# Attention in front of two expert layers on one core: array shapes of the attention matmuls

## The chip, the cores and the metric

One core of a Trainium2 chip runs the whole program. The metric is the device time of one execution in microseconds. Before the change three runs took 944.69, 947.47 and 947.21 us; their median is 947.21.

## The reference

Causal attention over 4 batches, 8 heads, 576 positions and head size 64, with a decay bias, then two feed-forward layers on the 2304 tokens:

```python
scores = scale * np.matmul(q, k.transpose(0, 1, 3, 2))
bias = -(cum[:, :, :, None] - cum[:, :, None, :])          # cum: running sum of max(s, 0)
scores = np.where(causal, -1000000000.0, scores + np.minimum(bias, 0.0))
attn = np.exp(scores - np.max(scores, axis=-1, keepdims=True))
attn = attn / (np.sum(attn, axis=-1, keepdims=True) + 1e-09)
x = np.matmul(attn, v)                                     # heads side by side: 2304 x 512
h = x @ w_in                                               # 512 -> 2048
x = (h * np.clip(h + 3.0, 0.0, 6.0) / 6.0) @ w_out         # 2048 -> 512
h = np.maximum(np.maximum(x @ w1, x @ w2), x @ w3)         # 512 -> 768
out = h @ w_out2                                           # 768 -> 512
```

All inputs are float32. The weights are decoded on the chip from 64-bit words.

## The kernel before, in words

The 576 queries of a head are cut into five chunks of up to 128; the last one, chunk 4, has 64 (n in the code). A "slot" (lines 839 to 927) handles one chunk of one head: TensorE (PE) makes its scores in PSUM (ps_s, line 865), the queries being the stationary operand and the keys the moving one; VectorE adds the causal mask and finds the row's extreme (line 886); ScalarE takes the exponential and sums the row (line 894); PE transposes the result in pieces of 128 keys (pt, line 916); ScalarE copies it to the tile e1p or e2p (batch 0) or e1, e2 (later batches). "average" (lines 929 to 976) multiplies it with the values (px, lines 948 and 955) for the first two chunks (group 0, 256 queries) or the last three (group 1, 320 queries). "reciprocals" turns the row sums into 1/sum and spreads each over 64 columns (ex); "finish" transposes that (pt_r, line 1014), multiplies the averages by it and stores the result (x_d). Two heads that lie side by side are a pair, and their averages are the two halves of 128 rows.

Batch 0 differs from the later ones. Its scores and averages are plain float32 matmuls, of which each shows as two records of PE in the trace. The later batches split every operand into a rounded float32 and its rest; a score there is two matmuls with one record each (128 and 66 rows), and an average has the rounded value and its rest side by side as 128 stationary columns. In batch 0 an average has the 64 values of one head as stationary columns. The scores of chunk 4 have 64 stationary columns in every batch, its transposes and the transposes of its reciprocals have 64 rows. All other matmuls use 128*128 or 66*128 (rows*columns of the stationary operand).

Between the attention's instructions PE does the first expert layer for tokens that are ready ("three", lines 484 to 488; ps_h and ps_x), and in the first 60 us some idle matmuls (line 574). The order of all instructions on every engine is fixed when the program is built: a planner (class Flow) runs the threads against costs that are written in the code (each `yield` with an engine and a cost) and emits an instruction when its engine comes free in the plan. On the chip each engine works through its list in order and waits on semaphores.

Rows of the sums that chunk 4 does not fill were set to 1 at the start (line 594), and the columns behind the 576 keys in chunk 4's tile e4 were set to 0 (line 596), on its 64 rows.

Of the kernel before, what the change touches and what calls it, by code (L numbers as in the profile page):

```python
# [15 lines left out]
AF = mybir.ActivationFunctionType  # L16
# [4 lines left out]
B, H, S, D = 4, 8, 576, 64  # L21
NT, DM, DFF, DF2 = B * S, 512, 2048, 768
P = 128
# [4 lines left out]
NCH = 5  # L28
U1 = S // 2
UCUT = ((0, 2 * P), (2 * P, S))  # L30
# [271 lines left out]
def attn_moe_moe2(ctx, tc, q, k, v, s, w_in, w_out, w1, w2, w3, w_out2, out):  # L302
# [187 lines left out]
    CHUNKED = ((0, 1), (2, 3, 4))  # L490
# [63 lines left out]
    def part_of(b, c):  # L554
        return min(1, c // 2) if b == 0 else 0
# [28 lines left out]
    def setup():  # L584
        make_identity(nc, ident)
        pool.memset(above, 0.0)
        pool.affine_select(
            out=above[:, 4 * P:], in_=above[:, 4 * P:], pattern=[[-1, P]],
            compare_op=ALU.is_ge, fill=MASK, base=0, channel_multiplier=1,
        )  # L590
        vec.memset(half, 0.5)
        for z in range(3):
            sums_of[z] = ap.tile([P, 2 * NCH], F32, tag=f"sums{z}", name="sums", bufs=1)
            vec.memset(sums_of[z], 1.0)
        e4 = ap.tile([P, NCH * P], F32, name="e4", bufs=1)
        pool.memset(e4[:S - 4 * P, S:], 0.0)
        et[0, "e4"] = e4
        et[0, 0] = ap.tile([P, 2, 2, 256], F32, tag="e1", name="e1p", bufs=1)
        et[0, 1] = ap.tile([P, 2, NCH, 320], F32, tag="e2", name="e2p", bufs=1)
        warm = psa.tile([P, P], F32, tag="t0", name="warm", bufs=1)  # L600
        for n in range(WARM):
            pe.matmul(warm, lhsT=ident, rhs=ident, start=(n == 0), stop=(n == WARM - 1))
# [236 lines left out]
    def slot(i, item, tiny):  # L839
        b, p, j, c = seq[i]  # L840
        h, pr = heads[b, p, j], pair[b, p, part_of(b, c)]
        n = min(P, S - c * P)
        qs = slice(c * P, c * P + n)
        soon = b == 0
        if soon:
            z, *tiles = yield early[part_of(b, c), p]
            o = c * P - UCUT[part_of(b, c)][0]
            passes = [(tiles[0][:, j, o:o + n], tiles[1][:, j])]
        else:
            passes = [(lhs[:, qs], rhs) for lhs, rhs in (yield h.ready)]  # L850
        w = min(S, (c + 1) * P)
        wp = (w + P - 1) // P * P
        e = et[0, "e4"] if c == NCH - 1 else make(item, [P, 512], F32, "e")
        cuts = [(0, 288), (288, 576)] if w > 512 else [(0, w)]
        parts = []
        for lo, hi in cuts:
            bank = yield S_.get()
            ps = make(bank, [P, 512], F32, "ps_s")
            o = ps[:n, 0:hi - lo]
            if soon:  # L860
                yield "PE", len(passes) * 4 * mm(hi - lo), False, i - AHEAD
            else:
                yield "PE", 2 * mm(hi - lo), False, i - AHEAD
            for x, (lhs, rhs) in enumerate(passes):
                pe.matmul(  # L865
                    o, lhsT=lhs, rhs=rhs[:, lo:hi],
                    start=(x == 0), stop=(x == len(passes) - 1),
                )
            parts.append((bank, ps, lo, hi))
        if soon:  # L870
            x = part_of(b, c), p
            early_left[x] -= 1
            if early_left[x] == 0:
                QK.put(z)
        else:
            h.scored += 1
            if h.scored == NCH:
                for st, it in h.release:
                    st.put(it)
        small = make((ap, f"tiny{tiny}"), [P, 4], F32, "tiny")  # L880
        m0 = 3.0e38
        shift = (NCH - 1 - c) * P
        for x, (bank, ps, lo, hi) in enumerate(parts):
            m = small[:n, x:x + 1]
            yield "DVE", dve2(hi - lo)
            vec.tensor_tensor_reduce(  # L886
                out=e[:n, lo:hi], in0=ps[:n, 0:hi - lo], in1=above[:n, shift + lo:shift + hi],
                scale=-0.125, scalar=m0, op0=ALU.add, op1=ALU.min, accum_out=m,
            )
            S_.put(bank)  # L890
            m0 = m
        r = sums_of[pr.sums][:n, 2 * c + j:2 * c + j + 1]
        yield "ACT", act1(w) + 0.186
        act.activation(  # L894
            e[:n, :w], e[:n, :w], AF.Exp, bias=m0, scale=-1.0, accum_out=r,
        )
        pr.left -= 1
        if pr.left == 0:
            pr.summed.set()
        TINY.put(tiny)  # L900
        g = 0 if c < 2 else 1
        if b > 0:
            yield et_real[g]
        if c in (0, 2):
            x = yield ET[g].get()
            h.et[g] = (x, et[min(b, 1), g])
            h.claimed[g].set()
        else:
            yield h.claimed[g]
        x, dst = h.et[g]  # L910
        o = (c if g == 0 else c - 2) * P
        bank = yield T.get()
        pt = make(bank, [P, c + 1, n], F32, "pt")
        yield "PE", 2 * mm(n) * (c + 1)
        for y in range(c + 1):
            pe.transpose(pt[:, y, :], e[:n, y * P:(y + 1) * P], ident[:n, :n])  # L916
        (E4 if c == NCH - 1 else E).put(item)
        dh = dst[:, x, 0:c + 1, o:o + n]
        yield from drained(dh, pt, n * (c + 1), ON["eh", b == 0])
        if b > 0:  # L920
            dl = dst[:, 1, 0:c + 1, o:o + n]
            yield "DVE", dve2(n * (c + 1))
            vec.tensor_tensor(out=dl, in0=pt, in1=dh.bitcast(F32), op=ALU.subtract)
        T.put(bank)
        h.count[g] += 1
        if h.count[g] == (2 if g == 0 else 3):
            h.full[g].set()

    def average(b, p, j, g):
        h, pr = heads[b, p, j], pair[b, p, g if b == 0 else 0]  # L930
        nj, o, n = GROUP[g]
        lo, hi = columns(b, g)
        if j == 0 and (b == 0 or g == 0):
            xi = yield X32.get()
            pr.x32.set((make(xi, [P, hi - lo], F32, "x32"), xi))
        x32, _ = yield pr.x32
        yield h.full[g]
        vhl = yield h.v
        y, src = h.et[g]
        bank = yield V.get()  # L940
        px = make(bank, [P, 512], F32, "px")
        xo = x32[j * D:(j + 1) * D, o - lo:o - lo + n]
        for x in range(nj):
            last = x == nj - 1
            z = max(0, x * P - o)
            if b == 0:
                yield "PE", 4 * mm(n - z), not last
                pe.matmul(  # L948
                    px[0:D, z:n], lhsT=vhl[:, x, j], rhs=src[:, y, x, z:n],
                    start=(x == 0), stop=last,  # L950
                )
            else:
                yield "PE", 2 * mm(n - z), not last
                for hl in range(2):
                    pe.matmul(  # L955
                        px[:, z:n], lhsT=vhl[:, x, j].rearrange("p l d -> p (l d)"),
                        rhs=src[:, hl, x, z:n], start=(x + hl == 0),
                        stop=(last and hl == 1),
                    )
        ET[g].put(y)  # L960
        pr.used[0] += 1
        if pr.used[0] == 8:
            pr.vrelease[0].put(pr.vrelease[1])
        if b == 0:
            yield from drained(xo, px[0:D, 0:n], n, ON["xo"])
        else:
            ui = yield UP.get()
            up = make(ui, [D, 320], F32, "up")
            yield from drained(up[:, 0:n], px[D:P, 0:n], n, ON["up"])
            yield "DVE", dve2(n)  # L970
            vec.tensor_tensor(out=xo, in0=px[0:D, 0:n], in1=up[:, 0:n], op=ALU.add)
            UP.put(ui)
        V.put(bank)
        pr.count += 1
        if pr.count == (2 if b == 0 else 4):
            pr.done.set()
# [22 lines left out]
    def finish(b, p, g):  # L999
# [6 lines left out]
        for y in ((g,) if b == 0 else (0, 1)):  # L1006
            _, o, size = GROUP[y]
            bank = yield T.get()
            ps = make(bank, [P, 512], F32, "pt_r")
            yield "PE", 2 * mm(size)  # L1010
            for c in CHUNKED[y]:
                m = min(P, S - c * P)
                wide = ex[0:m, 2 * c:2 * c + 2].rearrange("p j d -> p (j d)")
                pe.transpose(ps[:, c * P - o:c * P - o + m], wide, ident[0:m, 0:m])
            yield "DVE", dve2(size)
            xc = x32[:, o - lo:o - lo + size]
            vec.tensor_tensor(out=xc, in0=xc, in1=ps[:, 0:size], op=ALU.mult)
            T.put(bank)
# [818 lines left out]
```

## Time and profile before

| what | value |
|---|---|
| median of three runs | 947.21 us |
| the profiled execution | 943.51 us |
| its span, first to last instruction | 941.7 us |
| PE busy, share of the span | 98% |
| PE weight loads (PEld) | 91% |
| VectorE (DVE) | 71% |
| ScalarE (ACT) | 51% |
| GpSimd (POOL) | 33% |
| mean granted clock of PE | 0.998 |

The attention fills the first 345 us or so, batch 0 the first 121 of them; the rest is the expert layers. PE's records overlap: a matmul's record lasts until its result is out, so the start of the next one, or the piece in the chain of waits, tells its price, and not the record's length. The weight loads (PEld) run beside the matmuls. In forms, 128*64 128x320 is a stationary operand of 128 rows and 64 columns and a moving one of 128 rows and 320 columns.

### The profile page before, as it was taken

How to read it: one execution, taken by the hardware profiler on the slowest of the kernel's cores; microseconds unless marked ns; L12 is line 12 of the kernel's file. 1: busy time of each engine (PE TensorE's matmuls, PEld its weight loads, DVE VectorE, ACT ScalarE, POOL GpSimd, SP SyncE). 2: the span in 40 equal slices, each digit the busy share in tenths (PEclk: the TensorE clock that was granted, in tenths of full speed). 3: DMA queues.
4: the chain of work that ended last, by engine and by line, in shares of the span. 5: the costliest groups of instructions: out<-in, count | busy, mean ns of one | idle time of the engine just before them, and what ended most of it. 6: DMA issues, size and time to landing. Idle time of an engine off the chain costs nothing.

```text
span 941.7 us, 18963 instructions
## 1 busy us (share of the span) xinstructions
PE 922.3 (98%) x6630; PEld 859.8 (91%) x6630; DVE 671.7 (71%) x1661; ACT 479.7 (51%) x1220; POOL 307.0 (33%) x398
## 2 busy tenths in 40 slices
PE   9899999999999999999999999999999999999998
PEld 8545599988999999999999999999999999999998
DVE  5786477887878637885676887862857576777994
ACT  3666577768878645664354444542314232333552
POOL 4365354654744125554253444442000000000000
PEclk9999999999999999999999999999999999999999
DMA  5864567879877146663659788748742120283542
GB/s 153 216 175 110 129 158 201 215 202 256 224 202 206 62 149 190 210 211 109 193 204 312 242 282 311 262 172 291 253 141 64 50 78 32 75 306 100 159 146 76
DMA packets 94879, 167.80 MB, mean 178 GB/s; under 512 B 10144, under 2 KB 60840, under 8 KB 94784
## 3 DMA queue, kind: packets, MB, share of 16 engines
q1 hardware_dynamic: 94784, 166.60, 58.1%
q8 instruction: 52, 0.85, 0.4%
q14 instruction: 43, 0.35, 0.1%
HBM read 96.13 MB, written 49.17 MB: 154 GB/s over the span
## 4 chain that ended last, share of the span: by engine, by line
PE 79%; DMA 8%; DVE 6%; issue 2%; SPq 1%; ACT 1%; POOL 1%; DVEq 0%; POOLq 0%; ACTq 0%
PE ps_j L487 7%; PE ps_j L488 7%; PE ps_j L486 7%; PE ps_s L865 7%; PE ps_h L486 6%; PE ps_x L486 5%; PE ps_h L487 5%; PE ps_h L488 5%; PE ps_x L487 5%; PE ps_x L488 5%; PE pt L916 5%; PE px L955 3%; PE px L948 3%; PE ps_o L487 2%; DMA raw<-in_w_out_dram 2%
## 5 line engine op out<-in xcount | busy, mean ns | idle before, releaser
L486 PE MATMUL ps_h<-x,w 128*128 128x320 f32 (+1 forms) x512 | 157.5, 308 | 4.1 <-DVE g L1108 2.7
L486 PE MATMUL ps_x<-gt,w 128*128 128x320 f32 (+1 forms) x512 | 154.5, 302 | 2.0 <-DVE xf L1183 1.2
L487 PE MATMUL ps_x<-gt,w 128*128 128x320 f32 (+1 forms) x512 | 150.9, 295 | 0.3 <-POOL gt L385 0.2
L487 PE MATMUL ps_h<-x,w 128*128 128x320 f32 (+1 forms) x512 | 150.7, 294 | 0.0
L488 PE MATMUL ps_x<-gt,w 128*128 128x320 f32 (+1 forms) x512 | 150.6, 294 | 0.0
L488 PE MATMUL ps_h<-x,w 128*128 128x320 f32 (+1 forms) x512 | 150.5, 294 | 0.0
L385 POOL TENSOR_TENSOR gt<-g,gt 128x256 fp32r<-128x256 f32 (+1 forms) x107 | 86.9, 812 | 181.6 <-ACT gt L379 170.6
L487 PE MATMUL ps_j<-xf,wf 128*128 128x288 f32 x432 | 127.9, 296 | 0.0
L488 PE MATMUL ps_j<-xf,wf 128*128 128x288 f32 x432 | 127.6, 295 | 0.0
L486 PE MATMUL ps_j<-xf,wf 128*128 128x288 f32 x432 | 127.5, 295 | 0.0
L1104 ACT ACTIVATE u<-ps_h,half 128x256 f32<-128x256 f32 (+1 forms) x128 | 63.8, 498 | 98.5 <-PE ps_h L488 98.0
L894 ACT ACTIVATE e<-e,tiny 128x384 f32<-128x384 f32 (+4 forms) x160 | 96.0, 601 | 34.5 <-DVE tiny L886 33.5
L486 PEld LDWEIGHTS ps_h<-x,w 128*128 128x128 f32 x512 | 96.7, 189 | 11.9 <-issue 5.5
L865 PE MATMUL ps_s<-kt,qt 128*64 128x288 f32 (+9 forms) x384 | 102.8, 362 | 2.9 <-DMA kt<-in_k_dram 2.7
L1108 DVE SCALAR_TENSOR_TENSOR g<-u,ps_h 128x256 f32<-128x256 f32 (+1 forms) x128 | 57.6, 450 | 62.7 <-ACT u L1104 60.2
L486 PEld LDWEIGHTS ps_x<-gt,w 128*128 128x128 f32 x512 | 96.7, 189 | 3.3 <-DVE xf L1183 1.4
L886 DVE CUSTOM_DVE_ANT_0 e<-ps_s,above 128x384 f32<-128x384 f32 (+4 forms) x160 | 75.9, 477 | 30.1 <-PE ps_s L865 27.7
L487 PEld LDWEIGHTS ps_x<-gt,w 128*128 128x128 f32 x512 | 96.4, 188 | 0.7 <-POOL gt L385 0.7
L487 PEld LDWEIGHTS ps_h<-x,w 128*128 128x128 f32 x512 | 96.5, 188 | 0.1
L488 PEld LDWEIGHTS ps_x<-gt,w 128*128 128x128 f32 x512 | 96.5, 188 | 0.0
L488 PEld LDWEIGHTS ps_h<-x,w 128*128 128x128 f32 x512 | 96.4, 188 | 0.0
L379 ACT ACTIVATE gt<-g 128x256 fp32r<-128x256 f32 (+1 forms) x128 | 56.6, 442 | 56.7 <-DVE g L1108 54.9
(160 smaller groups left out, 2162.3 us busy)
## 6 DMA issues: line engine op xcount, KB each, us to landing
f_d<-wf SPq DMA_DIRECT2D x30, 512.0 KB
wf<-f_d SPq DMA_DIRECT2D x30, 512.0 KB
raw<-in_w_out_dram SPq DMA_DIRECT2D x22, 512.0 KB
kt<-kb SPq DMA_DIRECT2D x72, 144.0 KB
raw<-in_w_dram SPq DMA_DIRECT2D x18, 512.0 KB
x<-x_d SPq DMA_DIRECT2D x28, 320.0 KB
raw<-in_w_in_dram SPq DMA_DIRECT2D x16, 512.0 KB
x<-x_d SPq DMA_DIRECT2D x28, 256.0 KB
```

The lines of the kernel that those rows point to most:

```text
L379: act.activation(dst, src, AF.Copy)
L385: (pool if e == "POOL" else vec).tensor_tensor(out=dst, in0=a, in1=b_, op=ALU.subtract)
L486: pe.matmul(ps, lhsT=wh, rhs=xh, start=first, stop=False, skip_group_check=again)
L487: pe.matmul(ps, lhsT=wh, rhs=xl, start=False, stop=False, skip_group_check=again)
L488: pe.matmul(ps, lhsT=wl, rhs=xh, start=False, stop=last, skip_group_check=again)
L865: pe.matmul(o, lhsT=lhs, rhs=rhs[:, lo:hi], start=(x == 0), stop=(x == len(passes) - 1),)
L886: vec.tensor_tensor_reduce(out=e[:n, lo:hi], in0=ps[:n, 0:hi - lo], in1=above[:n, shift + lo:shift + hi], scale=-0.125, scalar=m0, op0=ALU ...
L894: act.activation(e[:n, :w], e[:n, :w], AF.Exp, bias=m0, scale=-1.0, accum_out=r,)
L916: pe.transpose(pt[:, y, :], e[:n, y * P:(y + 1) * P], ident[:n, :n])
L948: pe.matmul(px[0:D, z:n], lhsT=vhl[:, x, j], rhs=src[:, y, x, z:n], start=(x == 0), stop=last,)
L1104: act.activation(ut, ps, AF.Relu, bias=half, scale=1.0 / 6.0)
L1108: vec.scalar_tensor_tensor(out=g, in0=ut, scalar=1.0, in1=ps, op0=ALU.min, op1=ALU.mult)
```

## The change

Averages of batch 0 take the values of both heads as 128 stationary columns; the result has 128 rows, of which the half of the head in question is copied out. Chunk 4 is formed from the last 128 queries (448 to 575) instead of the last 64, through mask, exponential and sums; its transposes then read the upper 64 rows, with the lower right quarter of the identity. The reciprocals of chunk 4 are transposed from all 128 rows into the last 128 columns, ahead of chunks 2 and 3, whose transposes write over what they share. The padding of e4 is set to 0 on all rows. The costs in the `yield` lines stay as they are.

```diff
-        pool.memset(e4[:S - 4 * P, S:], 0.0)
+        pool.memset(e4[:, S:], 0.0)
...
-        qs = slice(c * P, c * P + n)
+        from_ = c * P + n - P
+        qs = slice(from_, from_ + P)
...
-            o = c * P - UCUT[part_of(b, c)][0]
-            passes = [(tiles[0][:, j, o:o + n], tiles[1][:, j])]
+            o = from_ - UCUT[part_of(b, c)][0]
+            passes = [(tiles[0][:, j, o:o + P], tiles[1][:, j])]
...
-            o = ps[:n, 0:hi - lo]
+            o = ps[:, 0:hi - lo]
...
-        shift = (NCH - 1 - c) * P
+        shift = (NCH - 1) * P - from_
...
-                out=e[:n, lo:hi], in0=ps[:n, 0:hi - lo], in1=above[:n, shift + lo:shift + hi],
+                out=e[:, lo:hi], in0=ps[:, 0:hi - lo], in1=above[:, shift + lo:shift + hi],
...
-        r = sums_of[pr.sums][:n, 2 * c + j:2 * c + j + 1]
+        r = sums_of[pr.sums][:, 2 * c + j:2 * c + j + 1]
...
-            e[:n, :w], e[:n, :w], AF.Exp, bias=m0, scale=-1.0, accum_out=r,
+            e[:, :w], e[:, :w], AF.Exp, bias=m0, scale=-1.0, accum_out=r,
...
-            pe.transpose(pt[:, y, :], e[:n, y * P:(y + 1) * P], ident[:n, :n])
+            pe.transpose(pt[:, y, :], e[P - n:, y * P:(y + 1) * P], ident[P - n:, P - n:])
...
-                    px[0:D, z:n], lhsT=vhl[:, x, j], rhs=src[:, y, x, z:n],
+                    px[:, z:n], lhsT=vhl[:, x].rearrange("p j d -> p (j d)"),
+                    rhs=src[:, y, x, z:n],
...
-            yield from drained(xo, px[0:D, 0:n], n, ON["xo"])
+            yield from drained(xo, px[j * D:(j + 1) * D, 0:n], n, ON["xo"])
...
-            for c in CHUNKED[y]:
-                m = min(P, S - c * P)
-                wide = ex[0:m, 2 * c:2 * c + 2].rearrange("p j d -> p (j d)")
-                pe.transpose(ps[:, c * P - o:c * P - o + m], wide, ident[0:m, 0:m])
+            for c in ((0, 1), (4, 2, 3))[y]:
+                at = min(c * P, S - P) - o
+                wide = ex[:, 2 * c:2 * c + 2].rearrange("p j d -> p (j d)")
+                pe.transpose(ps[:, at:at + P], wide, ident)
```

## Rows read from the trace of the kernel before

**Rows 1.** The page: the span and the engines' busy time.
```profile
span 941.7 us, 18963 instructions
PE 922.3 (98%) x6630; PEld 859.8 (91%) x6630; DVE 671.7 (71%) x1661; ACT 479.7 (51%) x1220; POOL 307.0 (33%) x398
```

**Rows 2.** Chain of waits, 0 to 56 us: start, length (us), what.
```profile
19.15 4.30 DMA kt<-in_k_dram
...
32.21 8.61 DMA kt<-in_k_dram
```

**Rows 3.** Busy time by stretch: from:to, length, us of each engine, clock, DMA.
```profile
41.00:55.00 14.00, 13.71 (x53) 6.68 (x54) 8.68 (x23) 8.27 (x22) 8.17 (x12) 0.88 0.95 244
55.00:70.00 15.00, 15.00 (x66) 7.28 (x66) 13.91 (x36) 9.46 (x23) 7.49 (x11) 1.00 0.46 136
...
80.00:121.00 41.00, 41.00 (x200) 22.48 (x200) 20.85 (x68) 24.32 (x65) 17.10 (x23) 1.00 0.49 117
...
180.00:240.00 60.00, 56.91 (x423) 51.88 (x421) 48.42 (x155) 46.30 (x131) 33.25 (x45) 1.00 0.86 234
```

**Rows 4.** Chain of waits, 56 to 92 us: start, length (us), what.
```profile
61.37 0.26 PE px L948 x2
...
62.51 0.63 PE ps_s L865 x2
63.14 0.54 PE px L948 x2
63.67 0.59 PE pt L916 x4
64.27 0.86 PE ps_s L865 x2
65.12 0.68 PE px L948 x2
65.81 0.31 PE ps_h L486
...
73.39 1.06 PE ps_s L865 x2
74.45 0.44 PE pt L916 x4
...
88.61 0.12 PE ps_h L486
```

**Rows 5.** Groups of PE by form, 0 to 345 us: busy us, mean ns.
```profile
L865 PE MATMUL ps_s<-kt,qt 128*64 128x288 f32 x80 | 27.9, 382 | 0.2 <-DVE tiny L886 0.2
...
L916 PE MATMUL pt<-ident,e 64*128 64x64 f32 x160 | 16.6, 232 | 0.7 <-DVE e L923 0.7
...
L1014 PE MATMUL pt_r<-ident,ex 64*128 64x64 f32 x16 | 4.4, 272 | 0.0
```

**Rows 6.** Chain of waits, 121 to 185 us.
```profile
141.54 0.22 PE pt_r L1014 x2
...
144.70 0.42 PE pt_r L1014 x3
145.12 0.37 PE pt L916 x2
```

**Rows 7.** Timeline of PE at 143 us: start, length, instruction.
```profile
143.22 0.28 PE L488 MATMUL ps_x<-gt,w 128*128 128x256 f32 x1
143.34 0.60 PE L865 MATMUL ps_s<-kt,qt 128*64 128x288 f32 x4
143.78 0.33 PE L486 MATMUL ps_x<-gt,w 128*128 128x256 f32 x1
```

**Rows 8.** Groups of VectorE by form, 0 to 345 us.
```profile
L886 DVE CUSTOM_DVE_ANT_0 e<-ps_s,above 64x288 f32<-64x288 f32 x32 | 14.1, 442 | 0.0
L886 DVE CUSTOM_DVE_ANT_0 e<-ps_s,above 128x256 f32<-128x256 f32 x32 | 13.4, 420 | 5.2 <-PE ps_s L865 4.4
```

**Rows 9.** Chain of waits, 181 to 236 us.
```profile
187.62 4.09 DMA x_d<-xs
```

More of the change, by code (lines that the diff above doesn't have):

```diff
@@ L881, in slot @@
         m0 = 3.0e38
-        shift = (NCH - 1 - c) * P
+        shift = (NCH - 1) * P - from_
         for x, (bank, ps, lo, hi) in enumerate(parts):
-            m = small[:n, x:x + 1]
+            m = small[:, x:x + 1]
             yield "DVE", dve2(hi - lo)
             vec.tensor_tensor_reduce(
-                out=e[:n, lo:hi], in0=ps[:n, 0:hi - lo], in1=above[:n, shift + lo:shift + hi],
+                out=e[:, lo:hi], in0=ps[:, 0:hi - lo], in1=above[:, shift + lo:shift + hi],
                 scale=-0.125, scalar=m0, op0=ALU.add, op1=ALU.min, accum_out=m,
```

## The prediction

> **What bounds the kernel now.** I read the page first: TensorE is busy 98% of the span [rows 1]. A busy PE says little here, because a record's time includes its latency. So I went to the chain of waits and read it piece by piece. A piece runs from the end of the record before it to its own end, so a piece of matmuls that is longer than their columns need holds something that no row names. Before 41 us two pieces are transfers of the first keys, 4.3 and 8.6 us long [rows 2]. From 41 to about 184 us nearly every piece is PE's, and all of those from 56 to 92 us are [rows 4]. The table by stretches shows who stands close behind: VectorE works 13.9 of the 15 us from 55 to 70, 20.9 of 41 from 80 to 121, and the DMA engines are 95% and 86% busy from 41 to 55 and from 180 to 240 [rows 3]. What the change is worth is therefore read in the chain of the first batch (15 to 121 us), and what may eat it in the other engines there.
>
> **What a change of array shape costs now.** The chain from 56 to 92 us shows the same work with and without a neighbour of another shape, written as stationary rows*columns [rows 4]. Two records of an average of 320 columns take 0.54 us behind narrow scores, which are 128*64 too, and 0.68 behind a wide score or a matmul of the expert layer. Two records of a score of 512 columns take 0.86 behind transposes of 128*128, 1.06 behind an average. The first of a triple of the expert layer takes 0.31 behind an average and 0.12 otherwise; four transposes 0.59 against 0.44. So on the way into the narrow shape 0.15 us are lost (0.68-0.54), on the way out 0.20 into a wide matmul (1.06-0.86, 0.31-0.12) and 0.15 into transposes. It is the change of shape and not that of line or kind: average behind narrow score changes the line and costs nothing.
>
> **Where this rule stops.** In batches 1 to 3 the scores of the last 64 queries are 128*64 and 66*64 as well, but in rounded float32 with one pass. There the step from an expert matmul into the narrow score takes 0.12 us (143.22 to 143.34), the pace of the triples, and four score records, narrow and wide, 0.44 where their 832 columns need 0.35 [rows 7]; no stall of 0.15 or 0.20 fits in. Making those 48 pairs wide saves nothing; each may show at most a longer weight load. I take 0.3 us in all, of a bound from 0 to 2.4 (48 at 0.05, the extra that the next part derives). The Trainium skill (TensorEngine Tiling (Array Packing), section Key Properties) says that changing the tiling mode drains TensorE and counts 64 columns as a mode. By its rule those 48 would stall too and widening them would give some 14 us more; the trace disagrees for this type [rows 7] and agrees for unrounded float32 [rows 4]. I go by the trace.
>
> **The change part by part.**
> (1) Averages of batch 0 with 128 stationary columns, and scores of the last queries formed as 128. I followed PE's order and counted the groups of narrow float32 records (112 of averages, 18.7 to 119.5 us, and 32 of scores, in the 80 records of the first row [rows 5]): 59 groups, entered and left once each. Nine of the entries come from a transpose of 64 rows, and one exit goes into one; the transposes of the last 64 queries keep 64 rows (160 records [rows 5]), so eight of these nine entries stay a change of shape (the ninth follows a reciprocal of 64 rows, part 2). By stretch, entries saved / exits into matmuls / exits into transposes: 15 to 41 us 10/8/2, 41 to 55 6/3/4, 55 to 70 8/8/1, 70 to 80 5/4/2, 80 to 121 21/19/7. With 0.15, 0.20 and 0.15 us these are 3.4, 2.1, 2.95, 1.85 and 8.0 us.
> What is added: a load of 128 columns where 64 were. Of the pieces named, 1.06 us is 0.86 and a stall s and a wide load; 0.68 is 0.54 and the same stall and a narrow load; the difference of 0.05 is the extra of a load that is not hidden. It shows where a change of shape stays (eight, 0.4 us in all: 0.05, 0.1, 0.05 and 0.2 from 41 us on) and where the moving columns are too few to hide it: the averages of 64 columns, 0.26 us a pair with 0.15 of stall in it [rows 4], so 0.11 bare, which I take as 0.21; eight of them, 0.8 us from 55 to 121 (0.2, 0.1, 0.5). Elsewhere 128 float32 columns and more pass behind each load and cover it. VectorE and ScalarE now work on 128 partitions instead of 64 for these scores. The mask step takes 442 ns on 64x288 and 420 on 128x256 [rows 8], the pace per column is the same, so 0; its cover, if wrong, is VectorE's idle time outside 55 to 70 us. The copy out of PSUM still moves 64 partitions, from the upper half for the odd head: 0, bounded by a tenth of a microsecond for each of eight odd pairs of copies either way.
> (2) Reciprocals on 128 rows: 16 transposes of 64*64 become 128*128 [rows 5] and come first of three. Three reciprocal transposes take 0.42 us with the narrow one and the two behind them 0.37; two plain ones take 0.22 [rows 6]. Three plain ones would be 0.33, two 0.22: 0.09 and 0.15, so 0.24 us a piece: 0.24 from 70 to 80, 0.48 from 80 to 121, 0.7 from 121 to 180, 1.0 from 180 to 235, 1.4 later.
> (3) The zeroing of the padding on all rows: once, before the first matmuls have data; 0.
> Nothing in the planner's costs is touched, so every engine and queue keeps its order but for the three reciprocal transposes among themselves.
>
> **The sum.** On PE: 15 to 41 us 3.4; 41 to 55 2.05; 55 to 70 2.7; 70 to 80 1.9; 80 to 121 7.8; batches 1 to 3 3.1-0.3; 20.6 in all. What of it comes out:
> 15 to 41 us: the ends are landings [rows 2]. Only that the second is issued a little earlier can help; I take 0.5 (bounds 0 and 3.4).
> 41 to 55: on the chain, but loads at 95% DMA come next: 1.7 (0 to 2.05).
> 55 to 70: VectorE has 1.1 us to spare [rows 3], and it will be late next, as its mask step gives PE the scores to transpose: 1.1 (0 to 2.7).
> 70 to 80: 1.9 (0.5 to 1.9). 80 to 121: VectorE 51%, ScalarE 59% busy; 6.6 of 7.8 (3.5 to 7.8), the rest for single waits that the stalls hid.
> Batches 1 to 3: 0.7 and 1.4 on the chain, the 1.0 from 180 to 235 lost behind stores and loads, less 0.3: about 1.8 (0 to 2.8).
> That is 13.6. It has to pass the stretch from 187 to 230 us, where the chain leaves PE for a store of 4.1 us, its successors on the queues, GpSimd and a load of keys [rows 9]. That chain starts from PE and moves with it, but 86% busy DMA engines will not take all of the earlier work at once: 1.4 us off. Behind it, expert matmuls follow with PE 98% busy and move as a whole. So 12.2 us: the profiled execution of 943.5 us (span 941.7) would come to 931.3. The median of the runs shown, 947.2, is 3.7 above that one; the same gain gives 935.0.
>
> **The rivals.**
> (a) Everything comes out: 20.6 us, 926.6. For it: all chain pieces are PE's from 56 to 92 us. Against: VectorE from 55 to 70, landings before 41.
> (b) Other engines take most of it back. Place: VectorE's fixed order from 55 to 121 us, where weight decoding and mask steps alternate, and landings before 55. If it is the bound as soon as PE hurries, 1.1 us remain up to 80, 2 of 7.8 later and 1 in batches 1 to 3: 4 us, 943. For it: 93% from 55 to 70. Against: 51% behind 80.
> (c) Slower: the stall belongs to the transition of operations and not to 64 columns, so it stays and only the wide load comes on top: 59 loads of 0.05 us behind stalls, 0.8 for the short averages and 0.5 for the rest: 4.3, so 951.5. It decides from the point where an average behind an expert matmul still takes 0.68 us or more. Against it: 0.54 behind narrow scores.
> (d) The rule by mode holds for the rounded scores too, hidden in a way that the timeline doesn't show: 48 exits and entries at some 0.30 give 14 more, about 921. The Trainium skill's page TensorEngine Tiling (Array Packing), Key Properties, speaks for it; the pace in rows 7 against it [rows 7].
>
> **How the numbers follow.** Forecast 0.62 (935, own range 930 to 940), (a) 0.14, (b) 0.15, (c) 0.05, (d) 0.04. Range 925 to 943.5: it holds the forecast, (a) and the greater part of (b), and leaves (c), (d) and the tail of (b) out. 0.3% is 2.8 us, what can be told from no change. Faster by more: forecast, (a), (d) and most of (b), 0.91; within: 0.05 (the poor end of (b)); slower: 0.04 (most of (c)).
>
> **What would show it.** Right: in the chain of the new kernel averages of 320 columns take 0.54 us a pair wherever they stand, 512-column scores 0.86, the first expert matmul behind them 0.12; only stalls around the 64-row transposes are left; the first batch ends 11 to 12 us earlier. VectorE near 100% or new PE waits for it between 55 and 70. Wrong: pairs of averages at 0.7 or more (c); PE waits of several us on VectorE or on loads before 121 us (b); the score pairs of batches 1 to 3 shorter by 0.3 us (d).

## The result, and the profile after

| | before | with the change |
|---|---|---|
| median on the first chip | 947.34 us (944.69 to 951.28) | 934.80 us (930.43 to 935.59) |
| median on a later chip, run again | 945.68 us (943.06 to 951.33) | 933.01 us (929.24 to 934.73) |
| ratio, 95% interval | | 0.9855 (0.9808 to 0.9902); again 0.986 (0.9829 to 0.989) |
| the profiled execution, its span | 943.51, 941.7 us | 935.59, 933.8 us |

The forecast was 935.0. The two profiled executions lie 7.9 us apart (9.6 in a second pair) and the medians 12.5: those of before (943.5, and 944.2 in a second profile) lie at the lower end of its runs, up to 951 us, and what the others spend no trace here shows; that stays open. It is not PE's clock: on another chip the kernel before took 943.54 and 951.0 us at mean granted clocks of 0.998 and 0.999. So the stages below are measured between fixed points of the traces and not from the span's start.

The page after, as in [rows 1]:

```profile
span 933.8 us, 18963 instructions
PE 907.6 (97%) x6630; PEld 872.4 (93%) x6630; DVE 668.8 (72%) x1661; ACT 478.5 (51%) x1220; POOL 307.0 (33%) x398
```

PE is still the bound, with more of its time in weight loads. The chain of waits of the changed kernel (start, length, what), where it is on PE again:

```profile
70.86 0.55 PE pt_r L1016 x3
71.41 0.54 PE px L949 x2
71.94 0.86 PE ps_s L866 x2
72.80 0.44 PE pt L917 x4
73.24 0.54 PE px L949 x2
73.78 0.12 PE ps_h L486
```

This is the picture of [rows 4] without its stalls: average pairs 0.54 us between reciprocals, wide scores, transposes and expert matmuls, 512-column scores 0.86 beside an average, four transposes 0.44 and the first expert matmul 0.12 behind one.

Up to 70 us the same chain shows what now ends last:

```profile
47.05 7.72 DMA raw<-in_w_out_dram
...
54.79 0.69 ACT ps_m L440
...
55.50 0.70 DVE ps_m L442
...
57.08 0.51 DVE e L887
```

The first raw block of the output weights lands at 54.8 us; behind it VectorE alternates decoding and mask steps, and the chain stays there until 69.6 us. The table by stretches, as in [rows 3] (the three last stretches moved to the same work):

```profile
55.00:70.00 15.00, 14.14 (x75) 10.16 (x74) 14.28 (x37) 11.10 (x26) 7.87 (x12) 1.00 0.50 143
70.00:80.00 10.00, 9.93 (x56) 7.32 (x55) 9.35 (x25) 7.36 (x19) 6.67 (x9) 1.00 0.73 202
80.00:112.00 32.00, 31.40 (x188) 25.15 (x187) 18.01 (x62) 22.12 (x59) 15.83 (x21) 1.00 0.55 136
...
171.00:231.00 60.00, 55.73 (x409) 52.11 (x408) 46.84 (x153) 44.96 (x128) 31.02 (x42) 0.97 0.82 225
```

VectorE works 14.3 of 15 us from 55 to 70 and 9.4 of 10 behind it; from 80 us on it has room again. The landing is not new on the chain: the chain of a second profile of the kernel before runs over it too.

```profile
45.94 7.53 DMA raw<-in_w_out_dram
```

The timeline of PE says where PE itself stands idle (start, length, instruction, idle time before it). These are its waits over 0.1 us from 55 to 112 us; the kernel before had none from 55 to 121 in the profile of [rows 1], and 1.2 us in its second one, behind the landing:

```profile
56.62 1.12 PE L866 MATMUL ps_s<-kt,qt 128*128 128x512 f32 x2 [0.52 <-DVE tiny L887]
58.62 0.52 PE L917 MATMUL pt<-ident,e 64*128 64x64 f32 x5 [0.34 <-ACT e L895]
...
90.41 0.52 PE L917 MATMUL pt<-ident,e 64*128 64x64 f32 x5 [0.54 <-ACT e2p L404]
```

**Stages between the same instructions.** The order on PE is the same in all kernels here but the one with late decoding (pieces of one group may be turned round), so the n-th record of PE can be compared. Four points were used: the start of ScalarE's first step on that raw block ("landing"), PE's expert matmuls that stand at 70.02, 121.10 and 345.01 us before, and the start of PE's last record. The timeline (start, length, instruction) of before and after has them as

```profile
54.04 0.64 ACT L440 ACTIVATE ps_m<-raw 128x512 f32<-128x512 f32 x1 [0.19 <-DMA raw<-in_w_out_dram]
...
70.02 0.39 PE L486 MATMUL ps_h<-x,w 128*128 128x256 f32 x1
...
121.10 0.28 PE L487 MATMUL ps_h<-x,w 128*128 128x256 f32 x1
```
```profile
54.79 0.68 ACT L440 ACTIVATE ps_m<-raw 128x512 f32<-128x512 f32 x1 [0.67 <-DMA raw<-in_w_out_dram]
...
68.83 0.36 PE L486 MATMUL ps_h<-x,w 128*128 128x256 f32 x1
...
111.83 0.28 PE L487 MATMUL ps_h<-x,w 128*128 128x256 f32 x1
```

| kernel (profile) | landing | landing to "70" | "70" to "121" | "121" to "345" | "345" to end |
|---|---|---|---|---|---|
| before | 54.04 | 15.98 | 51.08 | 223.91 | 593.2 |
| before, again | 53.50 | 15.98 | 51.08 | 224.39 | 594.0 |
| changed | 54.79 | 14.04 | 43.00 | 223.83 | 594.6 |
| changed, again | 54.67 | 14.02 | 42.99 | 223.30 | 594.4 |
| averages alone | 54.33 | 14.98 | 45.64 | 224.59 | 595.5 |
| last queries alone | 52.82 | 16.00 | 50.65 | 225.05 | 594.0 |
| narrow reciprocals | 52.92 | 14.01 | 43.54 | 225.10 | 593.7 |
| and narrow late scores | 54.63 | 14.00 | 43.59 | 224.65 | 594.4 |
| first group narrow | 51.83 | 14.01 | 43.04 | 222.75 | 594.1 |
| 96 columns | 54.39 | 14.00 | 43.02 | 222.95 | 592.8 |
| wide transposes | 53.76 | 13.93 | 42.91 | 222.40 | 594.8 |
| wide transposes, again | 52.51 | 13.90 | 42.79 | 223.56 | 595.7 |

Between two profiles of one kernel the first two stages repeat within 0.02 us (before, changed) or 0.12 (wide transposes), the later ones within 1.2; the landing lies anywhere from 51.8 to 54.8 us, in the changed kernel's two profiles no earlier than in those of before. Part of the scatter from "121" to "345" goes with PE's granted clock: from 180 to 240 us it was 1.00 in some profiles and 0.97, a piece of it at the lower level of 1.2 GHz, in others, whatever the kernel. The wide transposes took 222.40 us at 1.00 and 223.56 at 0.97, before 223.91 and 224.39 (stretches as above, first and second profile of the wide transposes):

```profile
180.00:240.00 60.00, 54.17 (x411) 51.42 (x411) 47.16 (x153) 45.17 (x129) 33.77 (x45) 1.00 0.83 222
```
```profile
180.00:240.00 60.00, 54.60 (x405) 51.98 (x404) 46.73 (x148) 45.56 (x129) 33.84 (x45) 0.97 0.84 224
```

By stages the change gains 1.95 us up to "70", 8.1 to "121", some 0.9 to "345" (mean 223.2 of the four profiles with the change's reciprocals and 64-row transposes against 224.15) and nothing that can be told behind it: 11 us of the 12.5 between the medians. Where the remaining 1.5 lie no stage shows; it is less than the landing's own scatter.

### The profile page after: what moved, and what is told of

Read it like the earlier page. It is cut to its first block, busy times and chain, and to the rows that moved or that the text cites. A ratio compares the mean times of both kernels' runs of the same rounds, so it can differ in the third digit from the quotient of the medians.

```text
span 933.8 us, 18963 instructions
## 1 busy us (share of the span) xinstructions
PE 907.6 (97%) x6630; PEld 872.4 (93%) x6630; DVE 668.8 (72%) x1661; ACT 478.5 (51%) x1220; POOL 307.0 (33%) x398
## 4 chain that ended last, share of the span: by engine, by line
PE 81%; DMA 8%; DVE 5%; ACT 2%; SPq 2%; issue 2%; POOL 1%; DVEq 0%; ACTq 0%; POOLq 0%
PE ps_j L487 7%; PE ps_j L486 7%; PE ps_j L488 7%; PE ps_h L486 7%; PE ps_x L486 6%; PE ps_x L487 6%; PE ps_x L488 6%; PE ps_h L487 6%; PE ps_h L488 6%; PE ps_s L866 5%; PE pt L917 4%; PE px L957 4%; PE ps_o L487 2%; PE ps_o L488 2%; PE ps_o L486 2%; DMA raw<-in_w_out_dram 2%
## 5 line engine op out<-in xcount | busy, mean ns | idle before, releaser
L866 PE MATMUL ps_s<-kt,qt 128*128 128x288 f32 (+9 forms) x384 | 102.8, 364 | 5.7 <-DMA kt<-in_k_dram 5.0
```

The source lines that it names most:

```text
L866: pe.matmul(o, lhsT=lhs, rhs=rhs[:, lo:hi], start=(x == 0), stop=(x == len(passes) - 1),)
```

## The experiments

Edits are shown against the changed kernel or, where it says so, against before. The ratio is to the kernel before on the same chip.

**Averages alone.** Only the two edits of "average", on the kernel before.

> Only the averages of batch 0 get 128 stationary columns; the last queries stay 64, the reciprocals as before. Theory (leaving and entering the 64-column float32 shape costs 0.15 us in and 0.15 to 0.20 out, once per group of narrow records in PE's order): of the 59 groups 41 hold averages alone and go, 13 hold averages and scores and stay as groups of scores, 5 are scores alone. From 55 to 121 us 28 of 42 go, so 6 to 6.5 us of the 9.4 that the whole change saved there; nothing for the reciprocals: 6 to 7 us faster than before, ratio 0.993. In the chain an average pair of 320 columns takes 0.54 us behind an expert matmul, but 0.6 or more next to a narrow score. Rival (the stall belongs to the step from one operation to another, the load of 128 columns comes on top): average pairs stay at 0.68 us or more and the time is 3 to 4 us above before.

939.24 us, ratio 0.9923 (0.9897 to 0.9949). From the chain of this kernel:

```profile
96.09 0.63 PE ps_s L865 x2
96.72 0.74 PE px L948 x2
...
98.66 0.54 PE px L948 x2
99.20 0.12 PE ps_h L486
```

The average behind a wide score has lost its stall (0.54, and 0.12 for the expert matmul behind it); the one behind a narrow score has got one it did not have, 0.74 against 0.54 [rows 4]. So the stall goes with the shape of the neighbour. From landing to "121" the gain is 6.4 us of the whole change's 10.0, as 28 of 42 groups would have it. The rival that the load alone would come on top is out.

**The last queries alone.** The change without its averages and with the reciprocals of the last queries transposed from the upper 64 rows.

> Only the last queries are formed as 128 (scores, mask, exponential, upper rows for the transposes; their reciprocals are transposed from the upper 64 rows); the averages of batch 0 stay at 64 columns. Theory (price per group): only the 5 groups that hold scores alone go, 3 of them before 55 us where transfers set the end; the 13 mixed groups stay as groups of averages. 0.5 to 1 us faster, ratio 0.999 to 1. Rival (price per narrow instruction): 16 narrow score pairs of batch 0 save 0.3 us each, 4 to 5 us, half of what the averages alone give. Second rival (mask and exponential on 128 rows cost time): slower by 1 us or more, and the mask step on 288 columns above 0.46 us.

944.24 us, ratio 0.9998 (0.9978 to 1.0017): nothing, as the price per group has it. Its chain:

```profile
87.49 0.48 PE ps_s L866 x2
87.97 0.68 PE px L949 x2
...
89.22 1.05 PE ps_s L866 x2
```

The score's stall is gone (0.48 for 0.63 [rows 4]), and the average behind it has it now (0.68 for 0.54). The parts don't add up: from landing to "121" they are 0.4 and 6.4 us alone and 9.5 together (the kernel with narrow reciprocals, next), because 13 groups held both. The 128 partitions cost next to nothing: the groups of the changed kernel by form show the mask step on 288 columns at 449 ns and the exponential at 775, against 442 [rows 8] and 773 before.

```profile
L887 DVE CUSTOM_DVE_ANT_0 e<-ps_s,above 128x288 f32<-128x288 f32 x32 | 14.4, 449 | 0.0
...
L895 ACT ACTIVATE e<-e,tiny 128x576 f32<-128x576 f32 x32 | 24.8, 775 | 13.9 <-DVE tiny L887 13.7
```

**Narrow reciprocals.**

```diff
-            for c in ((0, 1), (4, 2, 3))[y]:
-                at = min(c * P, S - P) - o
-                wide = ex[:, 2 * c:2 * c + 2].rearrange("p j d -> p (j d)")
-                pe.transpose(ps[:, at:at + P], wide, ident)
+            for c in CHUNKED[y]:
+                m = min(P, S - c * P)
+                wide = ex[P - m:, 2 * c:2 * c + 2].rearrange("p j d -> p (j d)")
+                pe.transpose(ps[:, c * P - o:c * P - o + m], wide, ident[P - m:, P - m:])
```

> The whole change without its last part: the reciprocals of the last queries are transposed as 64 rows (the upper ones), third of three as before. Theory: 16 pieces at 0.24 us come back, 13 of them behind 121 us; on the chain 0.7 us from 70 to 121, 0.7 from 121 to 180 and 1.4 behind 240, so 2 to 3 us slower than the whole change, ratio to before 0.988 to 0.989; three reciprocal transposes take 0.42 us in the chain against 0.33. Rival (hidden behind stores and loads in the later batches): under 1 us slower than the whole change.

935.61 us, ratio 0.9904 (0.9878 to 0.993). The chains, first of this kernel, then of the changed one:

```profile
134.21 0.42 PE pt_r L1016 x3
134.63 0.37 PE pt L917 x2
```
```profile
135.32 0.33 PE pt_r L1016 x3
135.65 0.22 PE pt L917 x2
```

0.24 us a piece, as worked out. In the stages 0.5 us from "70" to "121" (three pieces, two of them behind 80 us) and 1.3 to 2.3 up to "345": the 2 to 3 us that were expected, where the prediction had 0.72 for the first of these two stages.

**Narrow late scores.** Besides, the last queries of batches 1 to 3 are 64 columns again (rows, transposes and reciprocals on the lower 64).

```diff
-        from_ = c * P + n - P
-        qs = slice(from_, from_ + P)
+        rows = P if b == 0 else n
+        from_ = c * P + n - rows
+        qs = slice(from_, from_ + rows)
...
-            o = ps[:, 0:hi - lo]
+            o = ps[:rows, 0:hi - lo]
...
-                pt[:, y, :], e[P - n:, y * P:(y + 1) * P], ident[P - n:, P - n:])
+                pt[:, y, :], e[rows - n:rows, y * P:(y + 1) * P],
+                ident[rows - n:rows, rows - n:rows],
```

> As the kernel with narrow reciprocals, and in batches 1 to 3 the scores of the last queries are 64 columns as before the change, with their transposes and reciprocals on the lower 64 rows. Theory (a narrow shape in rounded float32 does not stall PE): the time of the kernel with narrow reciprocals within 1 us, ratio 0.988; PE from 121 to 345 us takes the same time within 0.5 us. Rival (the rule that every change of the tiling mode drains PE, at 0.30 us for each of 48 pairs): 14 us slower than the kernel with narrow reciprocals, as slow as before or slower. Second rival (a wide load shows behind transposes): up to 1 us faster than the kernel with narrow reciprocals.

936.46 us, ratio 0.9898 (0.9875 to 0.992), the same; from "121" to "345" 224.65 against 225.10. The 48 narrow pairs in rounded float32 cost no stall. The Trainium skill (TensorEngine Tiling (Array Packing), section Key Properties) says that a change of the tiling mode drains TensorE, and lists 128 rows by 64 columns among the modes. Taken so, it agrees with the plain float32 matmuls here (0.15 to 0.20 us a change [rows 4]) and not with these rounded ones.

**First group narrow.** Averages of the first two chunks of batch 0 (all that PE does before 55 us) with 64 columns.

```diff
-                    px[:, z:n], lhsT=vhl[:, x].rearrange("p j d -> p (j d)"),
+                    px[:, z:n] if g else px[0:D, z:n],
+                    lhsT=vhl[:, x].rearrange("p j d -> p (j d)") if g else vhl[:, x, j],
```

> The whole change, but the averages of the first two chunks in batch 0 (all of them before 55 us) keep 64 stationary columns. Theory (before 55 us the landings of keys and of the first late weights set the end, so stalls there are hidden): as fast as the whole change within 1 us, ratio 0.986 to 0.990; PE is as far at 55 us as with the whole change, give or take the 2 us by which landings differ from run to run. Rival (every group of narrow records costs its 0.35 us wherever it stands): 13 groups before 55 us, 4 to 5 us slower than the whole change, ratio 0.991 to 0.993.

934.50 us, ratio 0.9872 (0.9847 to 0.9898), like the whole change. Its raw block landed at 51.83 us, earlier than in any other profile here, and PE's point "70" came 14.01 us later, as everywhere. What PE saves before 55 us is worth nothing that these runs can tell, and the landing sets the end.

**96 columns.** Averages of even heads with 96 of the 128 columns.

```diff
-                    px[:, z:n], lhsT=vhl[:, x].rearrange("p j d -> p (j d)"),
+                    px[:, z:n] if j else px[0:96, z:n],
+                    lhsT=vhl[:, x].rearrange("p j d -> p (j d)")[:, 0:P if j else 96],
```

> The whole change, but the averages of the even heads take 96 of the 128 stationary columns. Theory (the stall hangs on the class of shape, 64 columns against more than 64): no stall comes back, average pairs of 320 columns stay at 0.54 us, time within 1 us of the whole change; where a load shows, behind a 64-row transpose or for averages of 64 columns, it is up to 0.03 us shorter. Rival (any other number of stationary columns than the neighbour's stalls): about half of the averages' groups come back, 0.68 us a pair, some 3 us slower than the whole change.

933.34 us, ratio 0.9866 (0.9846 to 0.9887). Its chain, with an odd head's pair of 128 columns at 94.26 and even heads' of 96 at 103.03 and 105.15; below it the instruction of the second from the timeline:

```profile
94.26 0.54 PE px L949 x2
94.80 0.12 PE ps_h L486
...
103.03 0.54 PE px L949 x2
103.58 0.12 PE ps_h L486
...
105.15 0.14 PE px L949 x2
```
```profile
102.87 0.70 PE L949 MATMUL px<-e2p,vf 128*96 128x320 f32 x2
```

No stall comes back: both heads take 0.54, and the expert matmul behind either 0.12. An even head's pair of 64 columns takes 0.14, where the changed kernel has 0.17 for the same pair: there the load shows and is shorter with 96 columns.

```profile
105.55 0.17 PE px L949 x2
```

**Wide transposes, twice.** The last 64-row matmuls of the attention go: the transposes of the last queries read 128 rows, from the last piece to the first.

```diff
-        pt = make(bank, [P, c + 1, n], F32, "pt")
+        back = c == NCH - 1
+        pt = make(bank, [P, c + 1 + back, n], F32, "pt")
...
-        for y in range(c + 1):
-            pe.transpose(pt[:, y, :], e[P - n:, y * P:(y + 1) * P], ident[P - n:, P - n:])
+        flat = pt.rearrange("p y n -> p (y n)")
+        for y in reversed(range(c + 1)) if back else range(c + 1):
+            pe.transpose(flat[:, y * n:y * n + P], e[:, y * P:(y + 1) * P], ident)
+        pt = pt[:, back:]
```

> The whole change, and the transposes of the last queries take all 128 rows too: five of 128*128 a piece, written from the last to the first so that each covers the columns that the one before it must not leave. No 64-row matmul is left in the attention. Theory: PE saves the step into 64 rows (0.09 to 0.10 us), the step out (0.13) and a shown load (about 0.1) for each of 32 pieces, and pays 5 x 0.046 us for the longer loads (109 against 63 ns from one transpose to the next): 0 to 0.1 us a piece, 0 to 3 us in all, ratio to before 0.983 to 0.987. Rival (the step between row modes is free like that of the rounded narrow scores, and only the loads count): 32 x 0.23 us, 5 to 7 us slower than the whole change.

> The kernel with 128-row transposes of the last queries once more, beside the whole change. Its first profile came from 121 to 345 us 1.4 us further ahead than that of the whole change, 0.06 us for each of 24 pieces. Theory (0 to 0.1 us a piece): 1 to 3 us faster than the whole change in its medians, and 1 to 1.5 us ahead of it from 121 to 345 us. Rival (the gain is swallowed behind stores and loads): the same time within 1 us.

933.10 us, ratio 0.9865 (0.9843 to 0.9886), and again 932.41, 0.9863 (0.9832 to 0.9893), beside 933.01 of the changed kernel on that chip. The five transposes and the average behind them, first here, then in the changed kernel:

```profile
96.23 0.55 PE pt L919 x5
96.78 0.33 PE px L952 x2
```
```profile
97.26 0.46 PE pt L917 x5
97.72 0.52 PE px L949 x2
```

0.88 us against 0.98: the 0.1 us a piece is there, and yet the stage from "70" to "121" gives 0.1 to 0.2, and from "121" the two profiles need 222.4 and 223.6 us where the changed kernel and its like had 222.8 to 223.8. The second run's rival was right: the same time within 1 us. Thus no version beats the changed kernel by an amount that these runs can tell.

**Late decoding.** `WO_AFTER = (1, 2)` in place of `(1, 0)`.

> The whole change, and the decoding of the first output weights (raw loads of 512 KB, VectorE chains) is allowed only when the third pair of group 1 has landed, two pairs later. The planner then writes another order. Theory (from 47 to 70 us the chain of the changed kernel runs over such a raw load and over VectorE's decoding, and PE waits): PE gains 1 to 2 us from 47 to 80 us more than with the whole change; 1 to 2 us faster than it if the later expert matmuls of batch 0 still find their weights. Rival (the decoding only moves the wait to 80 to 121 us, and PE has less expert work to fill with): as fast as the whole change or up to 4 us slower.

938.14 us, ratio 0.9915 (0.9895 to 0.9936), some 4 to 5 us slower than the whole change; the rival was right in size, or nearly, and not in place. Its order is another one, so it has no row in the table. PE works 59.3 of the 65 us from 175 to 240, against 60.7 in the changed kernel, and waits there for GpSimd, whose splitting of an expert input is late (waits of PE from 170 to 245 us in this kernel, and from 165 to 235 in the changed one: total, times, longest):

```profile
PE ps_x L487 <- POOL gt L385: 3.2, 1, 3.2
```
```profile
PE ps_x L487 <- POOL gt L385: 1.6, 2, 1.4
```

The longest of them, 3.2 us, ended at 221.05. From 220 to 231 us PE's granted clock was 0.53, close to the lower of its two levels (1.2 GHz), and the stretch reads:

```profile
220.00:231.00 11.00, 9.95 (x46) 9.61 (x47) 3.57 (x12) 3.71 (x10) 6.28 (x9) 0.53 0.65 187
```

This execution was the slowest of the six (942.83 us). Two others took 937.05 and 937.23 at mean clocks of 0.998 and 1.0, so the clock does not make the 4 us of the median, and the longer wait makes 1.6 of them between these two profiles; the rest stays open.

**Both kernels again.**

> The whole change once more, beside the kernel with wide transposes on the same chip. Expected ratio to before 0.985 to 0.989. Theory (the distance between two executions of one kernel arises before 55 us, in the landings of the first keys and weights): PE's place at 41 and 55 us differs by 1 to 3 us from the first profile of this kernel, but the time from 55 to 121 us is the same within 0.5 us (56.6 us for the work that took 66 before). Rival (the distance arises evenly or in the expert layers): the place at 55 us agrees within 0.5 us and the difference comes later.

> The kernel before once more, for a second profile. Theory: its landings before 55 us shift by 1 to 3 us against the first profile, its time from 55 to 121 us is 66 us within 0.5. Rival: more than 1 us of difference from 55 to 121 us, in which case the stretch's saving of 9.4 us is not the change's alone.

933.01 us, ratio 0.986 (0.9829 to 0.989), and 944.23 in one run. The second profile of before has the landing 0.54 us earlier, its first two stages are the same within 0.01 us. Both theories missed by their letter. The changed kernel's place at 55 us came out the same in both profiles (55.16 and 55.17). The kernel before had the PE record of 55.04 us at 53.15 in its second profile, so that from there to "121" it took 67.4 us and not 66.1: PE's place at 55 us is no fixed point, the landing is. That the landing moves by itself is shown by the kernel with narrow reciprocals, which does the same before 55 us as the changed one and has it 1.9 us earlier, and by the wide transposes, 53.76 and 52.51 in two profiles of one kernel.

## Why the prediction was right

The mechanism held piece by piece: 0.54, 0.86, 0.12 and 0.33 are the chain's lengths of the changed kernel, and rounded scores cost nothing. Two of its own signs came out short. The first batch was to end 11 to 12 us earlier; "121" came 9.3 and 8.9 us earlier in the two pairs of profiles, and 10.0 when measured from the landing. The profiled execution was to take 931.3 us and took 935.6, and 934.7 the second time. The terms of the sum compare as follows.

- 15 to 41 and 41 to 55 us, 0.5 and 1.7 taken: mis-sized, nothing came of them. What the kernel has at 55 us is a landing that PE's work does not move (54.04 and 53.50 us before, 54.79 and 54.67 after), and the narrow first group showed it. The prediction named the busy DMA there and still took most of the gain.
- 55 to 70 us, 1.1 with VectorE late next: the size was 1.95. Both kernels take a fixed time from the landing to "70", 15.98 and 14.04 us. In the changed kernel PE waits 0.86 us there for VectorE and ScalarE, all of it ahead of the five transposes at 58.62 (57.82 before): up to them both kernels take 3.8 us from the landing, and from them to "70" 12.2 and 10.2 without a wait of PE. So VectorE came close, busy 10.1 of these 10.2 us, and held PE up only behind the landing; its idle 1.1 us in [rows 3] was no ceiling. The three terms together were 3.3 and came out as 1.95.
- 70 to 121 us, 8.5 (1.9 and 6.6): 8.1. Of the full 9.7 there, 1.6 did not come. PE's new idle time is 0.67 us of it (0.07 and 0.60 in the table by stretches). Most of that, 0.54 us, ends a piece of 3.9 us in the chain of the changed kernel, over VectorE and ScalarE, where before the chain was on PE [rows 4]. Of the other 0.9 the reciprocals are 0.2 (0.5 in their own experiment, 0.72 taken), the rest was not traced to a term:

```profile
86.47 0.50 DVE e L887
...
87.38 1.03 DVE gt L385
...
89.06 0.81 ACT e L895 x2
89.87 0.49 ACT e2p L404
...
90.41 0.52 PE pt L917 x5
```

- The short averages: 0.21 us a pair taken, 0.17 in the pair shown above, 0.22 in another.
- Batches 1 to 3 and the passage behind them, 1.8 and -1.4: some 0.9 in place of 0.4, within the scatter of that stage. The toll of 1.4 us for busy DMA engines was not seen as such.

The sum was 12.2 us, the stages have 11 and the medians 12.5 and 12.7. That the total came out within 0.2 us of the median owes something to chance: the early terms were too large by 1.35 and the next by 0.4, the later batches too small by 0.5, and 1.5 us of the medians' distance lie in no stage. On the profiled execution the same sum missed by 4.3 us. Rival (a) fell to the landing and VectorE, (b) to the stage from 70 us on, (c) and (d) to the averages alone and the narrow late scores.

## What to carry to other kernels

Read PE's order for changes of the stationary operand's shape, price one way in and one way out from chain pieces with and without them, and count groups, not instructions: removing one of two neighbours in a group only moves the stall. Filling the array up to 128 columns costs nothing where the moving columns cover the load (0.54 us a pair of 320 moving columns with 96 and with 128; with 64 moving columns 0.14 and 0.17). A gain ahead of a fixed landing is worth nothing; measure stages from that landing.

## What the runs showed of the hardware that was not expected

- In plain float32 the stall hangs on 64 columns: 96 beside 128 had none (0.54 us a pair), 64 beside 128 had 0.15 on the way in and 0.15 to 0.20 on the way out.
- In rounded float32, 64 columns beside 128 had none: 48 pairs narrow or wide, 224.65 and 225.10 us for the stage.
- With unchanged order the two stages behind the landing repeat within 0.02 to 0.12 us in three kernels that were profiled twice, while the landing itself lies between 51.8 and 54.8 us in twelve profiles.
- From 180 to 240 us the granted clock of PE was 0.97 or 1.00, of one kernel too, and the stage around it 1.2 and 0.5 us longer at 0.97 in the two kernels seen at both.
